# MoE 2's first block of weights converted beside the last six attention chunks and kept in DRAM; first tokens transposed beside MoE 1's last steps

## The chip, the cores and the metric

One core of one Trainium2 chip runs the program. The metric is the device time of one execution in microseconds. The kernel uses TensorE (PE, with weight loads shown as PEld), VectorE (DVE), ScalarE (ACT), GpSimd (POOL) and the DMA queue that SyncE (SP) issues.

## The reference, cut to what matters

A linear-attention recurrence over 768 tokens for 4 batches of 8 heads of width 40, and then two feed-forward stages (called MoE 1 and MoE 2) over the 3072 resulting tokens of width 320. The weights `w_in`, `w_a`, `w_b` and `w_out` arrive as 64-bit floats, the rest as 32-bit.

```python
for t in range(S):
    y[:, :, t] = np.einsum('bhd,bhde->bhe', rt, state)
    Sa = np.einsum('bhde,bhe->bhd', state, at)
    state = state * wt - np.einsum('bhd,bhe->bhde', Sa, bt) + np.einsum('bhd,bhe->bhde', vt, kt)
...
h = x @ w_in                                   # MoE 1, d_ff 2048
x = (h * np.clip(h + 3.0, 0.0, 6.0) / 6.0) @ w_out
...
a = x @ w_a                                    # MoE 2, d_ff 1536
b = x @ w_b
out = a * b @ w_out
```

## The kernel before, in words

**Chunks.** The recurrence is done in 12 chunks of 64 steps, all 32 heads at once. `window(j)` (L697) lists the steps of chunk j by hand: small matmuls for chunk j, preparation for chunks j + 1 and j + 2, and between them two kinds of fillers, `MOE_STEP` and `WEIGHT`. The table `MOE` (L30 on) says before which steps of each window the MoE 1 steps stand. Each window from chunk 2 on has seven `WEIGHT` slots: after `merge_y`, after `op_d`, two around `st_copy`, after the first `op_f`, after the second `op_e`, and after `xt_move`. They call `conv1.go()` while MoE 1's own weights are being converted. That ends in chunk 1, so from chunk 2 on the slots do nothing.

Inside a chunk POOL inverts a triangular system with 62 instructions (`t_solve`, L507), started by `t_start(j + 1)` in window j. Its input comes from `op_a` (L472) on PE by way of two copies on ACT and two DRAM scratch transfers (`t_load`, L496). Behind the solve POOL multiplies the next chunk's `LB` (`prep_a`, L451), which the next window's `op_a` reads. `t_store` (L524) writes the solution to DRAM and reads it back, and `merge_y`, `merge_z`, `op_b` to `op_g` use it. `prep_w` (L444) and `prep_kb` (L461) run on DVE.

**MoE 1** works on 256 tokens per chunk (`moe1_stream`, L292): eight up steps and eight down steps per chunk, a down step one place behind its up step. An up step is 16 matmuls; ACT then makes the gate `g`, DVE multiplies, and `split` (L129) makes a rounded high part on ACT (`gh`) and the remainder on DVE (`gl`). A down step is 12 matmuls that read them. Of 192 steps 171 stand in the windows and 21 remain after the last chunk.

**64-bit weights** are turned into 32-bit by `to_f32` (L89): one activation on ACT, then five operations on DVE, and `split` adds a cast on ACT and a subtract on DVE. ACT and DVE each take their work in program order.

**After the last window** (L986 on) the attention's SBUF is given up, and MoE 2's pools open in it. A piece of MoE 2's weights is 256 columns (128 x 256 values, three per 128 rows of `d_ff`) or 160 columns (two per 128 rows); `Weights2` (L746) loads two pieces ahead (`ahead`) and converts one per `go`. `BLOCK` is 3, so the first block is 15 pieces. While the remaining MoE 1 steps run, each of them from the third on is followed by `w2.go(BLOCK - 1)`, so the first block is converted there. After the seventh step `decide` and the first load of MoE 2's tokens (`load_x(0)`) are issued. After the nineteenth come `trans(0)` (six PE transposes, with ACT and DVE making high and low parts), `load_x(1)`, the next-to-last step, `trans(1)`, and the last step. `load_x(0)` and `load_x(1)` use the same buffer. Then `rest()` (L890) runs MoE 2: four blocks of three rows of `d_ff`, six groups of 512 tokens each; it converts the next block's weights one piece per step.

SP issues all DMAs in program order, so a DMA that waits holds those behind it.

Of the kernel before, what the change touches and what calls it, by code (L numbers as in the profile page):

```python
# [8 lines left out]
F32 = mybir.dt.float32  # L9
F32R = mybir.dt.float32r  # L10
I32 = mybir.dt.int32
# [10 lines left out]
NCH = S // C  # L22
NP = 16
NT = B * S
DM = H * D
# [11 lines left out]
WEIGHTS = {  # L37
    0: (0, 3, 6, 8, 10, 17, 18, 21, 22, 22, 26, 27),
    1: (1, 2, 4, 5, 10, 13, 16, 16, 33, 36)}
STORE_1 = 25  # L40
WEIGHTS_2, RANGE = 2, 7
INV_SCALE = 1.0e9

HALVES = ((0, 0), (1, 64))
# [44 lines left out]
def to_f32(nc, st, c, h, p):  # L89
    for step in f32_steps(nc, st, c, h, p):  # L90
        step()
    return h.bitcast(F32)


def attention_and_moe(ctx, tc, t, flag):
    nc = tc.nc
    pe, ve, ac, gp, sp = nc.tensor, nc.vector, nc.scalar, nc.gpsimd, nc.sync
# [5 lines left out]
    dram = ctx.enter_context(tc.tile_pool(name="dram", bufs=1, space=DRAM))  # L103
# [13 lines left out]
    wk1 = m1.enter_context(tc.tile_pool(name="wk1", bufs=2))  # L117
# [11 lines left out]
    def split(hi, lo, src, eng=nc.vector):  # L129
        ac.copy(out=hi, in_=src)  # L130
        eng.tensor_tensor(out=lo, in0=src, in1=hi.bitcast(F32), op=ALU.subtract)  # L131

    def split_tail(dst, src, eng=nc.vector):
        ac.copy(out=dst, in_=src)
        eng.tensor_tensor(out=dst[64:128], in0=src[64:128], in1=dst[64:128].bitcast(F32), op=ALU.subtract)

    wide = t["w1i"].dtype != F32
    room = {"wide": True, "free": ["xt", "xh", "xl"], "live": set(), "lent": True, "n": 0}

    def words(src, dma):  # L140
        st = wk1.tile([128, 192, 2], I32, tag="ws", name="ws", bufs=3)[:, 0:src.shape[1]]
        dma.dma_start(out=st.rearrange("q c w -> q (c w)"), in_=src.bitcast(I32))
        return st

    def from_words(st):
        cv = wk1.tile([128, 2, 192], I32, tag="cv", name="cv2", bufs=2)[:, :, 0:st.shape[1]]
        return to_f32(nc, st, cv[:, 0], cv[:, 1], st[:, :, 1])

    class Converter:

# [24 lines left out]
    class Interleaved(Converter):  # L175


        x = y = z = None
# [41 lines left out]
    def load1(src, n, sink, c0):  # L220

        slot = None
        if room["wide"]:
            slot = room["free"].pop(0)
            room["live"].add(slot)
            if slot == "GH":
                st = GH.rearrange("q a p c -> q (a p c)")[:, 0:2 * n]
                sp.dma_start(out=st if not wide else st.bitcast(I32), in_=src.bitcast(I32) if wide else src)
                st = st.bitcast(I32).rearrange("q (c w) -> q c w", w=2) if wide else st
            else:  # L230
                st = stage_load(wk1, (slot, 0, 0, 0, 0, 1), src, n, sp)
        else:
            n = min(n, 192)
            st = words(src[:, 0:n], sp) if wide else stage_load(wk1, ("ws", 0, 0, 0, 0, 3), src[:, 0:n], n, sp)

        def steps():
            if not wide:
                yield from range(6)
                w = st
            elif slot:  # L240
                room["n"] += 1
                h = wk1.tile([128, n], I32, tag=("cv", "gh")[room["n"] % 2], name="cv_h", bufs=2)
                f32_steps(nc, st, h, h, h)[0]()
                yield
                p = wk1.tile([128, n], I32, tag="gl", name="cv_p")
                for step in f32_steps(nc, st, h, h, p)[1:]:
# [448 lines left out]
    WEIGHT, MOE_STEP = "weight", "moe"  # L695

    def window(j):  # L697
# [45 lines left out]
    NM = FF2 // 128  # L743
    BLOCK = 3

    class Weights2:  # L746


        def __init__(self, pool, stpool):
            self.pool, self.stpool, self.up, self.dn = pool, stpool, {}, {}  # L750
            self.todo = [(m, i) for m in range(NM) for i in range(5)]
            self.loaded = []

        def source(self, m, i):
            cols = slice(128 * m, 128 * m + 128)
            if i < 2:
                return [t[("w2a", "w2b")[i]][:, 0:2, cols]]
            if i == 2:
                return [t["w2a"][:, 2:3, cols], t["w2b"][:, 2:3, cols]]
            return [t["w2o"][:, m:m + 1, 160 * (i - 3):160 * (i - 2)]]  # L760

        def ahead(self):
            while self.todo and len(self.loaded) < 2:
                m, i = self.todo.pop(0)
                srcs = self.source(m, i)
                n = sum(x.shape[1] * x.shape[2] for x in srcs)
                k = 2 if wide else 1
                st = self.stpool.tile([128, 512], I32, tag="ws2", name="ws2", bufs=2)[:, 0:k * n]
                o = 0
                for x in srcs:  # L770
                    w = k * x.shape[1] * x.shape[2]
                    sp.dma_start(out=st[:, o:o + w].rearrange("q (k c) -> q k c", k=x.shape[1]), in_=x.bitcast(I32))
                    o += w
                self.loaded.append((m, i, st))

        def go(self, last):

            self.ahead()
            if not self.loaded or self.loaded[0][0] > last:
                return  # L780
            m, i, st = self.loaded.pop(0)
            if wide:
                st = st.rearrange("q (c w) -> q c w", w=2)
                cv = wk1.tile([128, 2, 256], I32, tag="cv", name="cv2", bufs=2)[:, :, 0:st.shape[1]]
                w = to_f32(nc, st, cv[:, 0], cv[:, 1], st[:, :, 1])
            else:
                w = st.bitcast(F32)
            if i == 0:
                self.up[m] = self.pool.tile([128, 10, 128], F32R, tag="up2", name="up2", bufs=2 * BLOCK)
            if i == 3:  # L790
                self.dn[m] = self.pool.tile([128, 2, DM], F32R, tag="dn2", name="dn2", bufs=2 * BLOCK)
            if i < 2:
                split(self.up[m][:, 4 * i:4 * i + 2], self.up[m][:, 4 * i + 2:4 * i + 4],
                      w.rearrange("q (k c) -> q k c", k=2))
            elif i == 2:
                split_tail(self.up[m][:, 8:10], w.rearrange("q (k c) -> q k c", k=2))
            else:
                cols = slice(160 * (i - 3), 160 * (i - 2))
                split(self.dn[m][:, 0, cols], self.dn[m][:, 1, cols], w)
            self.ahead()  # L800
# [114 lines left out]
    with tc.manual_schedule():  # L915
# [52 lines left out]
        def moe_step():  # L968
            mq.pop(0)()
            while mq and mq[0] in preps:  # L970
                mq.pop(0)()

        for j in range(NCH):
            for f in window(j):
                if f == MOE_STEP:
                    if j == 1 and mq[0] in preps:
                        mq.pop(0)()
                    else:
                        moe_step()
                elif f == WEIGHT:  # L980
                    if conv1.todo or conv1.loaded or room["wide"]:
                        conv1.go()
                else:
                    f[0](*f[1:])
        at.close()
        c2 = ctx.enter_context(ExitStack())  # L986
        w2p = c2.enter_context(tc.tile_pool(name="w2", bufs=1, side="right", reuse_waits="tile"))
# [2 lines left out]
        w2 = Weights2(w2p, xr)  # L990
        load_x, trans, rest = moe2(w2, xr, lambda: left[0])
        decide = in_range()
        w2.ahead()
        n = 0
        while len(mq) > 2:
            moe_step()
            n += 1
            if n > WEIGHTS_2:
                w2.go(BLOCK - 1)
            if n == RANGE:  # L1000
                decide()
                load_x(0)
        trans(0)
        load_x(1)
        m1i.close()
        mq.pop(0)()
        trans(1)
# [221 lines left out]
```

## Time and profile before

| | us |
|---|---|
| three runs | 1315.85, 1321.88, 1313.23; median 1315.85 |
| the profiled execution | 1317.48 |
| its span, first to last instruction | 1315.7 |
| its mean granted PE clock | 0.941 of full speed |

The span is what the trace's positions count in; the profiled execution's time is 1.8 us longer than its span. Busy shares of the span: PE 84%, DVE 60%, ACT 39%, POOL 38%. PEclk is the clock that TensorE was granted as a share of its full 2.4 GHz; 0.5 is the lower level.

### The profile page before, as it was taken

The page shows a single profiled execution, that of the slowest core. Times are in us where ns is not written, and L with a number is a line of the kernel's source. Part 1 is how long each engine was busy: PE and PEld are TensorE (multiplying, and loading weights), DVE is VectorE, ACT ScalarE, POOL GpSimd, SP SyncE. Part 2 cuts the span into 40 slices and gives each one's busy share as a digit, 9 for nine tenths or more (in the row PEclk, how much of TensorE's full clock was granted, in tenths as well). Part 3 has the DMA queues.
Part 4 walks back from the last instruction along what each step waited for, and adds up shares of the span by engine and source line. Part 5 has one row for each costly group of instructions (what it writes and reads, how often), then busy time and mean ns, then how long its engine had stood idle before and what let it go on. Part 6 is the DMA issues. An engine that isn't in the chain of part 4 may idle for free.

```text
span 1315.7 us, 34806 instructions
## 1 busy us (share of the span) xinstructions
PE 1106.6 (84%) x14826; PEld 1010.3 (77%) x14826; DVE 793.0 (60%) x1371; ACT 516.7 (39%) x1087; POOL 502.1 (38%) x817
## 2 busy tenths in 40 slices
PE   1213347998999899898989999778999999999997
PEld 1213336898989889898989899777888888888886
DVE  7899867473746557373746334575765675675333
ACT  1242344454554545354544644333343232232221
POOL 4789205665858484756748570000000000000000
PEclk9999657898999899999989999988999999999999
DMA  6253251324151423323141321222220110110111
GB/s 176 49 143 99 67 161 42 98 63 100 56 133 37 114 69 92 91 61 100 56 120 36 89 59 41 64 74 88 82 74 24 35 43 26 35 43 11 40 40 44
DMA packets 128770, 94.43 MB, mean 72 GB/s; under 512 B 87040, under 2 KB 117888, under 8 KB 126592
## 3 DMA queue, kind: packets, MB, share of 16 engines
q1 hardware_dynamic: 128608, 92.14, 26.1%
q8 instruction: 118, 1.93, 0.6%
q14 instruction: 44, 0.36, 0.1%
HBM read 72.18 MB, written 19.92 MB: 70 GB/s over the span
## 4 chain that ended last, share of the span: by engine, by line
PE 45%; POOL 24%; DVE 12%; DMA 7%; issue 6%; ACT 4%; SPq 1%; POOLq 0%; DVEq 0%; ACTq 0%
PE att L847 20%; POOL TN L519 11%; POOL TT L516 10%; PE up L309 6%; PE ac L871 3%; PE ac L870 3%; PE ac L869 3%; POOL LB L454 3%; DMA TA<-scr 2%; PE att L482 1%; PE dn L329 1%; DMA scr<-AB 1%; PE dn L331 1%; PE dn L330 1%; DVE cv_p L78 1%
## 5 line engine op out<-in xcount | busy, mean ns | idle before, releaser
L516 POOL TENSOR_TENSOR TT<-TA,TN 64x31 f32<-64x31 f32 (+15 forms) x372 | 207.9, 559 | 228.5 <-DMA TA<-scr 200.1
L847 PE MATMUL att<-x2h,up 128*128 128x512 f32 x720 | 237.4, 394 | 0.0
L519 POOL TENSOR_TENSOR TN<-TN,TT 64x31 f32<-64x31 f32 (+15 forms) x372 | 218.2, 586 | 29.2
L847 PE MATMUL att<-x2l,up 128*128 128x512 f32 x432 | 170.7, 395 | 2.0 <-DVE x2l L832 2.0
L847 PEld LDWEIGHTS att<-x2h,up 128*128 128x128 f32 x720 | 135.4, 188 | 29.0
L329 PE MATMUL dn<-wo_h,gh 128*128 128x320 f32 x384 | 129.4, 337 | 17.4 <-ACT gh L130 17.4
L315 DVE SCALAR_TENSOR_TENSOR up<-g,up 128x512 f32<-128x512 f32 x96 | 66.5, 693 | 117.6 <-ACT g L314 117.6
L314 ACT ACTIVATE g<-up,bias 128x512 f32<-128x512 f32 x96 | 66.0, 687 | 167.1 <-PE up L309 164.0
L331 PE MATMUL dn<-wo_h,gl 128*128 128x320 f32 x384 | 122.7, 320 | 1.1 <-DVE gl L131 1.0
L330 PE MATMUL dn<-wo_l,gh 128*128 128x320 f32 x384 | 121.3, 316 | 0.0
L309 PE MATMUL up<-xh,wi_h 128*128 128x256 f32 x384 | 113.0, 314 | 3.1 <-ACT xh L288 3.1
L852 DVE TENSOR_TENSOR att<-att,asb 128x512 f32<-128x512 f32 x72 | 50.4, 700 | 98.0 <-PE att L847 80.8
L309 PE MATMUL up<-xh,wi_l 128*128 128x256 f32 x384 | 107.0, 298 | 0.0
L131 DVE TENSOR_TENSOR gl<-up,gh 128x512 fp32r<-128x512 f32 x96 | 66.4, 691 | 62.5 <-ACT gh L130 62.5
L130 ACT CAST gh<-up 128x512 fp32r<-128x512 f32 x96 | 56.2, 586 | 102.7 <-DVE up L315 102.7
L847 PEld LDWEIGHTS att<-x2l,up 128*128 128x128 f32 x432 | 81.2, 188 | 19.4 <-DVE x2l L832 3.5
L482 PE MATMUL att<-LB,KB 40*64 40x64 f32 x1408 | 40.8, 275 | 63.9 <-POOL LB L454 30.9
L329 PEld LDWEIGHTS dn<-wo_h,gh 128*128 128x128 f32 x384 | 74.4, 194 | 22.4 <-ACT gh L130 18.9
L869 PE MATMUL ac<-dn,g2h 128*128 128x320 f32 x288 | 89.5, 311 | 0.0
L482 PEld LDWEIGHTS att<-LB,KB 40*64 40x64 f32 x1408 | 35.4, 185 | 70.4 <-POOL LB L454 34.4
L871 PE MATMUL ac<-dn,g2l 128*128 128x320 f32 x288 | 88.6, 308 | 0.1
L870 PE MATMUL ac<-dn,g2h 128*128 128x320 f32 x288 | 88.7, 308 | 0.0
(146 smaller groups left out, 2549.4 us busy)
## 6 DMA issues: line engine op xcount, KB each, us to landing
RV<-in_rve_dram SPq DMA_DIRECT2D x24, 320.0 KB
KB<-in_kbe_dram SPq DMA_DIRECT2D x22, 320.0 KB
st<-in_w1i_dram SPq DMA_DIRECT2D x13, 384.0 KB
raw<-in_we_dram SPq DMA_DIRECT2D x24, 162.5 KB
LB<-in_ae_dram SPq DMA_DIRECT2D x24, 160.0 KB
VX<-in_vte_dram SPq DMA_DIRECT2D x24, 160.0 KB
yt<-Y SPq DMA_DIRECT2D x48, 80.0 KB
x2d<-x SPq DMA_DIRECT2D x24, 160.0 KB
```

What stands on the lines that cost most here:

```text
L309: mm(u[:, e], a_, b_, start=(n == 0), stop=(n == len(seq) - 1))
L315: ve.scalar_tensor_tensor(out=uf, in0=g, scalar=6.0, in1=uf, op0=ALU.min, op1=ALU.mult)
L329: mm(acc, gh[:, e, c0:c0 + 128], wo_h[:, m], start=(m == 0), stop=False)
L330: mm(acc, gh[:, e, c0:c0 + 128], wo_l[:, m], start=False, stop=False)
L331: mm(acc, gl[:, e, c0:c0 + 128], wo_h[:, m], start=False, stop=(m == 15))
L482: mm(pss[ab][half(c), i], KB[rows(ab), p, 64 * c:64 * c + 64], lb[rows(ab), ab, p], start=True, stop=True)
L516: eng.tensor_tensor(out=tv, in0=TA[:, 0:u, u:u + 1].to_broadcast([nr, u, n]), in1=TN[:, u:u + 1, u:32].to_broadcast([nr, u, n]), op=ALU.mult)
L519: eng.tensor_tensor(out=TN[:, 0:u, u:32], in0=TN[:, 0:u, u:32], in1=tv, op=ALU.subtract)
L847: mm(u, a_, b_, start=(n == 0), stop=(n == len(seq) - 1))
L869: mm(acc, gh[:, sl], w[:, 0], start=(i == 0), stop=False)
L870: mm(acc, gh[:, sl], w[:, 1], start=False, stop=False)
L871: mm(acc, gl[:, sl], w[:, 0], start=False, stop=(i == BLOCK - 1))
```

## The change

`WEIGHT` slots of windows 6 to 11 (`EARLY = NCH - 6`) no longer call `conv1.go()`. Of the seven slots of each of these windows the first, fourth and seventh advance a generator, `early2()`. Its first call loads piece 0; each later call converts the loaded piece, splits it into high and low parts that overwrite the loaded words, stores them to a DRAM tensor `made2`, and loads the next piece. After the windows `Weights2` reads all 15 pieces of the first block from `made2` straight into their places. The conversion loop beside MoE 1's last steps is gone, and `trans(0)` and `load_x(1)` are issued after the twelfth of these steps, not after the nineteenth. The staging tile `ws` gets 256 columns and two buffers in place of 192 columns and three, and the work tile `cv` one part in place of two.

```diff
+EARLY = NCH - 6
+WCOLS = 256
-WEIGHTS_2, RANGE = 2, 7
+RANGE = 7
...
-        st = wk1.tile([128, 192, 2], I32, tag="ws", name="ws", bufs=3)[:, 0:src.shape[1]]
+        st = wk1.tile([128, WCOLS, 2], I32, tag="ws", name="ws", bufs=2)[:, 0:src.shape[1]]
...
-        cv = wk1.tile([128, 2, 192], I32, tag="cv", name="cv2", bufs=2)[:, :, 0:st.shape[1]]
-        return to_f32(nc, st, cv[:, 0], cv[:, 1], st[:, :, 1])
+        h = wk1.tile([128, WCOLS], I32, tag="cv", name="cv2", bufs=2)[:, 0:st.shape[1]]
+        return to_f32(nc, st, h, h, st[:, :, 1])
...
+    made2 = dram.tile([BLOCK * PIECES, 128, 512], F32, name="made2")
...
+    def early2():
+
+        todo = [(m, i) for m in range(BLOCK) for i in range(PIECES)] if wide else []
+        st = load2(wk1, "ws", 2 * WCOLS, *todo[0]) if wide else None
+        yield
+        for n, (m, i) in enumerate(todo):
+            w = f32_2(st)
+            c = w.shape[1]
+            hi, lo = st[:, 0:c].bitcast(F32R), st[:, c:2 * c].bitcast(F32R)
+            if i == 2:
+                split_tail(hi, w)
+                sp.dma_start(out=made2[n, :, 0:c].bitcast(I32), in_=st[:, 0:c])
+            else:
+                split(hi, lo, w)
+                sp.dma_start(out=made2[n, :, 0:2 * c].bitcast(I32), in_=st)
+            if n + 1 < len(todo):
+                st = load2(wk1, "ws", 2 * WCOLS, *todo[n + 1])
+            yield
...
+            while wide and self.todo[0][0] < BLOCK:
+                m, i = self.todo.pop(0)
+                self.room(m, i)
+                src = made2[PIECES * m + i]
...
+                sp.dma_start(out=dst.bitcast(F32), in_=src)
...
+        first2, early = early2(), [0] * NCH
...
+                elif f == WEIGHT and j >= EARLY:
+                    early[j] += 1
+                    if early[j] in (1, 4, 7):
+                        next(first2, None)
...
+        for _ in first2:
+            pass
         at.close()
...
-        w2.ahead()
         n = 0
         while len(mq) > 2:
             moe_step()
             n += 1
-            if n > WEIGHTS_2:
-                w2.go(BLOCK - 1)
             if n == RANGE:
                 decide()
                 load_x(0)
-        trans(0)
-        load_x(1)
+            if n == RANGE + 5:
+                trans(0)
+                load_x(1)
```

## Rows read from the trace of the kernel before

**Rows 1.** The page, part 2: PE's busy tenths in 40 slices.
```profile
PE   1213347998999899898989999778999999999997
```
**Rows 2.** Windows view: stretch, PE, PEld, DVE, ACT, POOL busy (instructions), PEclk, DMA share, GB/s.
```profile
742.00:827.00 85.00, 85.00 (x1609) 81.17 (x1608) 32.96 (x50) 38.13 (x67) 32.73 (x62) 1.00 0.19 48
...
831.00:904.00 73.00, 53.05 (x307) 49.31 (x307) 49.36 (x122) 25.11 (x56) 0.00 (x0) 0.82 0.24 72
...
682.00:742.00 60.00, 56.78 (x1085) 53.77 (x1085) 34.63 (x47) 30.08 (x64) 40.03 (x66) 0.97 0.31 74
...
830.00:835.00 5.00, 5.00 (x39) 5.00 (x39) 2.24 (x4) 1.84 (x4) 0.00 (x0) 1.00 0.63 184
```
**Rows 3.** Waits from 831 to 904 us: total us, times, longest.
```profile
PE dn L329 <- ACT gh L130: 16.5, 7, 6.3
```
**Rows 4.** Timeline of PE: start, length, instruction, [idle before and releaser].
```profile
827.30 0.28 PE L309 MATMUL up<-xh,wi_h 128*128 128x256 f32 x1
...
829.22 0.31 PE L329 MATMUL dn<-wo_h,gh 128*128 128x320 f32 x1
...
830.98 0.28 PE L309 MATMUL up<-xh,wi_h 128*128 128x256 f32 x1
...
838.93 0.42 PE L329 MATMUL dn<-wo_h,gh 128*128 128x320 f32 x1 [0.43 <-ACT gh L130]
...
843.14 0.28 PE L309 MATMUL up<-xh,wi_h 128*128 128x256 f32 x1
...
851.61 0.64 PE L329 MATMUL dn<-wo_h,gh 128*128 128x320 f32 x1 [6.27 <-ACT gh L130]
...
890.34 0.82 PE L828 MATMUL att<-ident,xin 128*128 128x128 f32 x6
...
904.17 0.63 PE L847 MATMUL att<-x2h,up 128*128 128x512 f32 x1
```
**Rows 5.** Timeline of ACT: the cast that ends a weight piece.
```profile
845.37 0.40 ACT L130 CAST up<-cv 128x256 fp32r<-128x256 f32 x1 [2.07 <-DVE cv L86]
```
**Rows 6.** The chain that ended last, in order of time: start, length, what.
```profile
668.48 2.16 POOL LB L454
...
728.43 2.15 POOL LB L454
```
**Rows 7.** PE's waits from 682 to 742 us, the only row.
```profile
PE att L482 <- POOL LB L454: 3.2, 2, 1.9
```
**Rows 8.** Timeline of ACT, chunk 9: the evictions of `merge_z`.
```profile
691.54 1.20 ACT L562 ACTIVATE AB<-att 32x512 f32<-32x512 f32 x2 [1.90 <-PE att L559]
```
**Rows 9.** Timeline of POOL: first and last instructions of solves.
```profile
91.32 0.34 POOL L516 TENSOR_TENSOR TT<-TA,TN 64x31 f32<-64x31 f32 x1
...
134.61 0.25 POOL L519 TENSOR_TENSOR TN<-TN,TT 64x31 f32<-64x31 f32 x1
...
688.97 0.34 POOL L516 TENSOR_TENSOR TT<-TA,TN 64x31 f32<-64x31 f32 x1 [14.89 <-DMA TA<-scr]
...
747.39 0.26 POOL L516 TENSOR_TENSOR TT<-TA,TN 64x31 f32<-64x31 f32 x1 [13.47 <-DMA TA<-scr]
...
784.64 0.25 POOL L519 TENSOR_TENSOR TN<-TN,TT 64x31 f32<-64x31 f32 x1
```
**Rows 10.** DVE groups by form, 91.3 to 134.9 us: busy us, mean ns, idle before.
```profile
L447 DVE TENSOR_TENSOR_SCAN W<-raw,seg 128x260 f32<-128x260 f32 x4 | 3.7, 926 | 0.0
...
L263 DVE TENSOR_TENSOR wi_t<-cv_h,wi_t 64x384 fp32r<-64x384 f32 x1 | 0.9, 854 | 0.0
```
**Rows 11.** DVE groups by form, 689 to 728.5 us.
```profile
L465 DVE TENSOR_TENSOR KB<-KB,rw 128x512 f32<-128x512 f32 x4 | 3.4, 860 | 1.0 <-DMA KB<-in_kbe_dram 1.0
...
L447 DVE TENSOR_TENSOR_SCAN W<-raw,seg 128x260 f32<-128x260 f32 x3 | 2.4, 785 | 0.0
```
**Rows 12.** Tile `ws`, 831 to 904 us: ns min/median/max, first and last start.
```profile
L80 DVE SCALAR_TENSOR_TENSOR cv<-cv,ws x15: 324/425/428, 840.8 to 894.4; 128x256 int32<-128x256 int32 x9, 128x160 int32<-128x160 int32 x6
...
L772 SPq DMA_DIRECT2D ws<-in_w2a_dram x7: 341/378/527, 830.7 to 891.3; - x7
```

More of the change, by code (lines that the diff above doesn't have):

```diff
@@ L233, in load1 @@
             n = min(n, 192)
-            st = words(src[:, 0:n], sp) if wide else stage_load(wk1, ("ws", 0, 0, 0, 0, 3), src[:, 0:n], n, sp)
+            st = words(src[:, 0:n], sp) if wide else stage_load(wk1, ("ws", 0, 0, 0, 0, 2), src[:, 0:n], n, sp)
         def steps():
@@ L744, in attention_and_moe, with source2, load2, f32_2 @@
     BLOCK = 3
+    PIECES = 5
+    made2 = dram.tile([BLOCK * PIECES, 128, 512], F32, name="made2")
+    def source2(m, i):
+        cols = slice(128 * m, 128 * m + 128)
+        if i < 2:
+            return [t[("w2a", "w2b")[i]][:, 0:2, cols]]
+        if i == 2:
+            return [t["w2a"][:, 2:3, cols], t["w2b"][:, 2:3, cols]]
+        return [t["w2o"][:, m:m + 1, 160 * (i - 3):160 * (i - 2)]]
+    def load2(pool, tag, room_, m, i):
+        srcs = source2(m, i)
+        k = 2 if wide else 1
+        st = pool.tile([128, room_], I32, tag=tag, name=tag, bufs=2)[:, 0:k * sum(x.shape[1] * x.shape[2] for x in srcs)]
+        o = 0
+        for x in srcs:
+            w = k * x.shape[1] * x.shape[2]
+            sp.dma_start(out=st[:, o:o + w].rearrange("q (k c) -> q k c", k=x.shape[1]), in_=x.bitcast(I32))
+            o += w
+        return st
+    def f32_2(st):
+        if not wide:
+            return st.bitcast(F32)
+        st = st.rearrange("q (c w) -> q c w", w=2)
+        h = wk1.tile([128, WCOLS], I32, tag="cv", name="cv2", bufs=2)[:, 0:st.shape[1]]
+        return to_f32(nc, st, h, h, st[:, :, 1])
+    def early2():
[6 more added lines that the diff above has]
+            hi, lo = st[:, 0:c].bitcast(F32R), st[:, c:2 * c].bitcast(F32R)
+            if i == 2:
+                split_tail(hi, w)
[6 more added lines that the diff above has]
+            yield
     class Weights2:
@@ L750, in __init__, with room @@
             self.pool, self.stpool, self.up, self.dn = pool, stpool, {}, {}
-            self.todo = [(m, i) for m in range(NM) for i in range(5)]
+            self.todo = [(m, i) for m in range(NM) for i in range(PIECES)]
             self.loaded = []
[L754 to L760, printed above, removed]
+            while wide and self.todo[0][0] < BLOCK:
+                m, i = self.todo.pop(0)
+                self.room(m, i)
+                src = made2[PIECES * m + i]
+                if i < 2:
+                    dst, src = self.up[m][:, 4 * i:4 * i + 4], src.rearrange("q (k c) -> q k c", c=128)
+                elif i == 2:
+                    dst, src = self.up[m][:, 8:10], src[:, 0:256].rearrange("q (k c) -> q k c", c=128)
+                else:
+                    dst = self.dn[m][:, :, 160 * (i - 3):160 * (i - 2)]
+                    src = src[:, 0:320].rearrange("q (k c) -> q k c", k=2)
+                sp.dma_start(out=dst.bitcast(F32), in_=src)
+        def room(self, m, i):
+            if i == 0:
+                self.up[m] = self.pool.tile([128, 10, 128], F32R, tag="up2", name="up2", bufs=2 * BLOCK)
+            if i == 3:
+                self.dn[m] = self.pool.tile([128, 2, DM], F32R, tag="dn2", name="dn2", bufs=2 * BLOCK)
         def ahead(self):
@@ L764, in ahead @@
                 m, i = self.todo.pop(0)
[L765 to L774, printed above, removed]
+                self.loaded.append((m, i, load2(self.stpool, "ws2", 512, m, i)))
         def go(self, last):
@@ L781, in go @@
             m, i, st = self.loaded.pop(0)
[L782 to L791, printed above, removed]
+            w = f32_2(st)
+            self.room(m, i)
             if i < 2:
```

## The prediction

> **What bounds the kernel now.** I read the page's forty slices first. TensorE is near full from slice 8 on, except for a dip at slices 26 to 28 (busy tenths 7, 7, 8; each slice is 32.9 us) [rows 1]. The windows view puts numbers on the two stretches around it: from 742 to 827 us, the last two chunks, PE is busy all 85 us, but from 831 to 904 us, the last 21 steps of MoE 1, it is busy 53.05 of 73 us and its granted clock averages 0.82 [rows 2]. The waits of that stretch have one owner: the down steps waited 16.5 us for the cast `gh` [rows 3]. PE's timeline shows the pattern. Undisturbed, a down step takes 829.22 to 830.98, that is 1.76 us, and an up step 827.30 to 829.22, 1.92 us. With weight pieces between a gate's cast and its input, the first down step of the last chunk comes 6.27 us late, and its matmuls then take 0.64 us, not 0.31: the lower of the clock's two levels [rows 4]. On ACT a piece holds the in-order queue: after its first activation (as long as its cast, 0.40 us) ACT stands 2.07 us until DVE's fifth operation is done and then casts for 0.40 us, 2.9 us in all [rows 5].
>
> In the chunks before, something else ends last. The chain of waits runs through a ring: POOL's `LB` product, `op_a` on PE, an up step, the scratch DMAs into `TA`, then POOL's solve until the next `LB` product. One turn is 668.48 to 728.43, 59.95 us [rows 6]. PE is 95% busy there (56.78 of 60 us [rows 2]) but waits 3.2 us a chunk, only for `LB` [rows 7]. So in chunks 6 to 9 PE has 3.2 us to give away, and POOL and the ring have nothing.
>
> **The change, part by part.**
>
> *1. Fifteen pieces leave the tail.* I rebuild PE's order without them. Up to 843.14 + 1.92 = 845.06 nothing changes. Then follow down 0 (1.76 us, plus 0.9 us because only one up step stands between its input and itself; the same kind of spot costs 0.43 us at 838.93 [rows 4]), so 847.7; six up steps (11.5 us); seven down steps (12.3 us); and the transposes of the first two token blocks, twice 0.82 us [rows 4]. Sum: 873.1. MoE 2's first matmul stood at 904.17 [rows 4], so it comes 31.0 us earlier. That matmul and the next few ran at the lower clock (0.63 us for one); without an idle stretch ahead I count another 0.7 us. Together 31.7 us.
> What hides the rest of this stretch: ACT and DVE keep only the gates; their chain from an up step's end to `gl` fits in the 3.68 us of the next pair, as it does without a wait at 829 us. If that cover failed, a pair would cost some 0.4 us more, 3 us in all.
>
> *2. Fifteen reloads.* They are issued on SP right behind the last tokens' own load: 15 x 0.38 us [rows 12] = 5.7 us of SP, 2.95 MB. The tokens stand ahead of them, the store of MoE 1's chunk 10 and the first load of `x2d` behind. At the 184 GB/s that the queue reached at 830 to 835 us [rows 2] they need 16 us and are in by 847; the first transposes come at about 855, MoE 2 at 873. Cost 0. If they only went at the stretch's mean of 72 GB/s [rows 2] they would take 41 us, and the first transposes would be 17 us late. I take the peak row, because it was measured for the same kind of load back to back, and the mean only shows what was asked for.
>
> *3. The first transposes in the loop.* The six matmuls are counted above. `load_x(1)` shares their buffer and can start at about 856; `trans(1)` stands at about 870, so there are 14 us for one load. Cost 0; before, it cost an idle stretch. The first pieces of the second block are no longer loaded ahead, but only in MoE 2's second step; their conversion stands behind that step's evictions and the next tokens' casts on ACT, and what it makes is needed five groups later: cost 0, at most one wait for a load, on ACT alone.
>
> *4. The pieces in the chunks: PE.* Per chunk three slots are used, after `merge_y`, ahead of `op_f` and behind `xt_move`; the first `next` only loads, so chunk 6 gets two pieces, chunks 7 to 10 three, chunk 11 one. Behind `merge_y` ACT's next work is the evictions of `merge_z`, which started after 1.90 us of idle [rows 8]; a stay of 2.9 us makes them 1.0 us late, and `op_c` with them. At the other two slots ACT and DVE have idle time of that size and PE other work. So PE arrives about 1 to 1.5 us later at `op_a`, where it waits 3.2 us anyway: cost 0 in chunks 6 to 9. In chunks 10 and 11 no wait is left [rows 2]: two first slots, at most 2 x 1.0 us; I take 0.5. If all fifteen stays landed on the chain it would be 15 x 2.9 = 43 us.
>
> *5. The pieces in the chunks: POOL.* This is the term that decides. Every piece puts four DVE operations with two inputs in SBUF (`L80`, `L84`, `L86` and the split's subtract; 0.425 us each at 256 columns [rows 12]) beside POOL's solve, and POOL is in the ring. The trace shows three solves of the same 62 instructions. With next to no such operations it takes 747.39 to 784.64 + 0.25, 37.50 us. With seven more of them (four `L465`, three `L447`, 5.8 us [rows 11]) it runs from 688.97 [rows 9] to the `LB` product at 728.43 [rows 6], 39.46 us: 2.0 us more, 0.28 us per operation. Beside MoE 1's conversion, with 35 of them in 30.1 us (thirteen groups, the first and the last of them in [rows 10]), it takes 91.32 to 134.86, 43.54 us: 6.0 us more, 0.17 us per operation [rows 9]. So a piece costs POOL 4 x 0.17 = 0.7 to 4 x 0.28 = 1.1 us; by busy time (6.0 / 30.1 = 0.20 and 2.0 / 5.8 = 0.34, times 1.7 us) it is 0.34 to 0.58 us. I take 0.7, the middle. Eleven pieces stand beside a solve that the ring waits for (two in chunk 6, three each in 7, 8, 9): 7.7 us, bounds 3.7 and 12.3. The solve of chunk 10 is the last, and its end is followed by steps that wait for ACT: 0.
> The Trainium skill (SBUF — State Buffer, "Who interferes with whom") says that a VectorE instruction with two SBUF inputs and a GpSimd one that reads SBUF exclude each other, and that the loser blocks for the whole instruction. The rows agree that there is a price, but 0.17 to 0.28 us is a fraction of those operations' lengths (about 0.85 us). By the rule at its fullest the term would be 18.7 us in place of 7.7.
>
> *6. The pieces in the chunks: SP.* Each slot's store waits for the split, with the next load behind it. At the third slot `load_rv`, the next chunk's loads and `t_store` are queued behind; 2 x 0.38 us a chunk over four chunks is 3.2 us at most. PE waits for none of what these bring [rows 7], so I take 0.
>
> *7. Two `ws` buffers in place of three, one `cv` half in place of two.* Only seven pieces of MoE 1 use them before; a load there may wait for one conversion. Between 0 and 0.6 us; I take 0.
>
> Sum: -31.7 + 7.7 + 0.5 = -23.5 us. The profiled execution took 1317.48 us, so 1294.0 on its own scale; the median of the three runs, 1315.85, is 1.6 us lower, and so is the forecast: **1292.4 us**.
>
> **The rivals.**
> - *The chunks hide everything* (POOL's loss stays near 0, or PE's later arrival at `op_a` saves what POOL loses, since the up step there runs at the lower clock after the wait): 1292.4 - 7.7 = 1284.7. For it: DVE is only 58% busy in a chunk (34.63 of 60 us [rows 2]). Against: the three solves.
> - *POOL loses the whole length of each such operation*: 4 x 0.425 = 1.7 us a piece, 11 x 1.7 = 18.7, so 1303.4. For it: the gap between 37.50 and 39.46 exists at all. Against: 35 operations of 0.86 us cost 6.0 us, not 30.
> - *The reloads are slow* and the first transposes wait: +17, so 1309. Against: 184 GB/s in the row.
> - *Slower: ACT's stay lands on the ring or on PE each time.* Place: ACT's queue at the three slots. Price: 2.9 us x 15 = 43 us against 31.7, so 1315.85 + 11.8 = 1328. It decides from 31.7 / 15 = 2.1 us a piece. For it: a stay of 2.9 us in an in-order queue, which did cost the tail 6.27 us once; Against: in the tail several pieces stood together, here one stands alone among steps that leave 3.2 us a chunk.
> - *It doesn't do what it says*: 18 slots for 16 calls leave no remainder for after the chunks, so only if the tail were bound by something else: 1315.
>
> **How the numbers follow.** A measurement of this kernel can tell about 1%, 13.2 us, from no change. Chances: forecast 0.57, all hidden 0.21, full lock 0.11, slow reloads 0.04, slower 0.05, nothing 0.02. Faster by over 1% means below 1302.7: the forecast, all hidden, and half of the full lock, 0.57 + 0.21 + 0.06 = 0.84. Within 1%: the other half, slow reloads, nothing, 0.11. Slower 0.05. The range reaches from just under the hidden case, 1283, to the full lock, 1304; its ends also cover part 5's bounds (1288 to 1297) with parts 4, 6 and 7 at their dearest.
>
> **What would show it.** In the changed profile: no wait on `gh` over 1 us between the last chunk and MoE 2, that stretch some 42 us long, at full clock; solves of chunks 7 to 9 about 2 us longer than 39.5 and a ring of about 62 us; PE still waiting for `LB` only. Wrong would be: solves as before (then 1285), new waits on `AB` or `VX` in chunks 10 and 11, or on `xin` or the reloaded weights ahead of MoE 2.

## The result, and the profile after

The kernel after takes 1301.39 us (median of 8 runs, 1299.54 to 1306.14), the kernel before 1315.06 us (8 runs): 0.9896 of it, 95% interval 0.9873 to 0.9918. That is 13.7 us faster; the forecast had 23.5. The change's profiled execution took 1300.71 us, its span is 1298.9 us. The page's slices of PE (the kernel after):

```profile
PE   1213347998999898989899999999999999999997
```

The dip of [rows 1] at slices 26 to 28 is gone. The windows view of the kernel after, with columns as in [rows 2] (one turn of the ring, the last two chunks, and MoE 1's last steps):

```profile
690.00:752.00 62.00, 57.59 (x1094) 53.81 (x1094) 43.81 (x65) 32.16 (x70) 40.10 (x66) 1.00 0.38 94
...
754.00:839.00 85.00, 81.66 (x1486) 77.36 (x1486) 40.47 (x71) 39.27 (x73) 34.53 (x62) 0.98 0.23 62
...
845.00:888.00 43.00, 41.91 (x312) 40.61 (x311) 19.30 (x33) 15.71 (x26) 0.00 (x0) 1.00 0.34 104
```

PE's waits of the last of these stretches, which answer to [rows 3]:

```profile
PE dn L331 <- ACT gh L132: 0.6, 2, 0.4
...
```

PE's timeline there, the first tokens' transposes and MoE 2's first matmul, which answer to the last two of [rows 4]:

```profile
869.76 0.82 PE L872 MATMUL att<-ident,xin 128*128 128x128 f32 x6
...
888.04 0.39 PE L891 MATMUL att<-x2h,up 128*128 128x512 f32 x1
```

The tail did what was forecast: 16.5 us of waiting for `gh` became 0.6, PE is busy 41.91 of 43 us at full clock, and MoE 2's first matmul takes 0.39 us in place of 0.63. In the chunks DVE has 9 us more to do in a turn (43.81 against 34.63), and PE, which waited for nothing but `LB` there [rows 7], now waits for other engines too. Its waits from 690 to 752 us, the turn that answers to that of [rows 7]:

```profile
PE att L484 <- POOL LB L456: 2.5, 2, 1.9
PE att L639 <- DVE GH L618: 0.5, 2, 0.3
PE att L655 <- ACT VX L592: 0.5, 1, 0.5
...
```

**Where the time went.** I cut the ring into two parts by POOL's timeline: a *solve*, from the first to the last of its 62 instructions, and the *leg* from its end to the next solve's start (`LB` product, `op_a`, `t_store`, `t_load`). The pieces stand beside the five solves of chunks 6 to 10 and in the legs between them; the table adds up these five solves and the five legs that lead into them. The two rows in which one such solve begins and ends in the kernel after (chunk 8) show how each is read; the bracket says what POOL waited for:

```profile
636.32 0.25 POOL L518 TENSOR_TENSOR TT<-TA,TN 64x31 f32<-64x31 f32 x1 [18.53 <-DMA TA<-scr]
...
676.20 0.25 POOL L521 TENSOR_TENSOR TN<-TN,TT 64x31 f32<-64x31 f32 x1
```

So this solve took 40.13 us, and the leg before it ran from 612.3, the end of the solve before, to 636.32, 24.0 us. Read so in every profile (us; MoE 2's start by the chain that ended last; the times are medians, the ratios to the kernel before on the same chip):

| kernel | five solves, chunks 6 to 10 | legs into them | last solve to MoE 2 | MoE 2 starts | time | ratio |
|---|---|---|---|---|---|---|
| before | 195.2 | 100.5 | 119.5 | 904.4 | 1315.06 | 1 |
| after | 200.1 | 107.0 | 90.6 | 888.2 | 1301.39 | 0.9896 |
| *first chip* | | | | | | |
| e1, no pieces | 195.7 | 98.5 | 88.2 | 871.3 | 1285.19 | 0.9771 |
| e2, transfers alone | 195.5 | 101.0 | 91.1 | 876.8 | 1291.77 | 0.9824 |
| e3, no stores | 201.2 | 100.8 | 90.3 | 877.3 | 1295.05 | 0.9849 |
| e4, third slot earlier | 197.8 | 129.4 | 94.4 | 909.6 | 1321.18 | 1.0041 |
| *second chip* | | | | | | |
| f1, store kept back | 198.6 | 114.9 | 93.9 | 895.8 | 1307.26 | 0.9924 |
| f2, two slots, 8 chunks | 197.5 | 107.6 | 90.9 | 887.1 | 1298.00 | 0.9850 |
| f3, transposes late | 199.9 | 104.3 | 92.6 | 886.6 | 1301.52 | 0.9882 |
| f4, DVE additions alone | 204.8 | 103.0 | 86.0 | 882.3 | 1298.11 | 0.9852 |
| *third chip* | | | | | | |
| g1, `xt` loads later | 199.6 | 105.1 | 90.0 | 885.6 | 1293.94 | 0.9834 |
| g2, g1 and f2 | 198.1 | 98.0 | 89.4 | 879.1 | 1287.07 | 0.9771 |
| g3, after once more | 200.0 | 105.4 | 95.0 | 888.1 | 1296.91 | 0.9847 |
| g4, f2 once more | 198.1 | 101.7 | 90.3 | 881.6 | 1296.40 | 0.9850 |

The kernel after gains 28.9 us behind the last solve (119.5 to 90.6) and 0.6 in MoE 2, and gives back 4.9 in the solves, 6.5 in the legs and 1.3 ahead of the first of these legs: 16.8 us, the difference of the spans.

One plain limit of this table: the same kernel's ratio was 0.9896 (0.9873 to 0.9918) at first and 0.9847 (0.9824 to 0.9869) on the third chip, the legs of one kernel differ by up to 6 us between two profiles (f2 and g4), and its last stretch by 4.4 (after and g3). So times are compared within one chip's group, and a leg counts where the queue's rows say why it is long.

### The profile page after: what moved, and what is told of

It is laid out like the page before. It is cut to its first block, busy times and chain, and to the rows that moved or that the text cites. A ratio compares the mean times of both kernels' runs of the same rounds, so it can differ in the third digit from the quotient of the medians.

```text
span 1298.9 us, 34813 instructions
## 1 busy us (share of the span) xinstructions
PE 1103.0 (85%) x14826; PEld 1006.5 (77%) x14826; DVE 807.8 (62%) x1371; ACT 518.0 (40%) x1087; POOL 507.6 (39%) x817
## 4 chain that ended last, share of the span: by engine, by line
PE 43%; POOL 19%; DVE 13%; DMA 11%; ACT 6%; issue 5%; SPq 2%; POOLq 0%; DVEq 0%; ACTq 0%
PE att L891 21%; POOL TN L521 8%; POOL TT L518 8%; PE up L311 6%; PE ac L915 3%; PE ac L914 3%; PE ac L913 3%; POOL LB L456 2%; DMA scr<-AB 2%; DMA TA<-scr 2%; DMA KB<-in_kbe_dram 2%; PE att L484 2%; DVE rw L451 1%; DMA st<-in_w1o_dram 1%; PE dn L333 1%
## 5 line engine op out<-in xcount | busy, mean ns | idle before, releaser
L521 POOL TENSOR_TENSOR TN<-TN,TT 64x31 f32<-64x31 f32 (+15 forms) x372 | 222.4, 598 | 29.2
L484 PE MATMUL att<-LB,KB 40*64 40x64 f32 x1408 | 38.1, 261 | 59.5 <-POOL LB L456 26.2
L451 DVE RECIPROCAL rw<-W 128x256 f32<-128x256 f32 x48 | 84.2, 1753 | 3.2 <-ACT sq L461 0.2
L484 PEld LDWEIGHTS att<-LB,KB 40*64 40x64 f32 x1408 | 32.8, 172 | 65.9 <-POOL LB L456 29.5
```

The costliest lines, as they stand in the source:

```text
L451: ve.reciprocal(out=rw, in_=w[:, :, 1:65])
L484: mm(pss[ab][half(c), i], KB[rows(ab), p, 64 * c:64 * c + 64], lb[rows(ab), ab, p], start=True, stop=True)
L521: eng.tensor_tensor(out=TN[:, 0:u, u:32], in0=TN[:, 0:u, u:32], in1=tv, op=ALU.subtract)
```

## What lengthens a leg

SP's queue at the chunk's end, in the timeline of the kernel before (start, length, line, transfer; the solve ends at 609.7):

```profile
606.21 0.83 SPq L435 DMA_DIRECT2D RV<-in_rve_dram  x2
...
608.23 0.67 SPq L427 DMA_DIRECT2D LB<-in_ae_dram  x2
609.70 0.31 SPq L532 DMA_DIRECT2D n<-TN  x1
...
612.38 0.32 SPq L534 DMA_DIRECT2D n<-TA  x1
616.09 0.32 SPq L538 DMA_DIRECT2D NY<-n  x1
...
618.57 0.49 SPq L540 DMA_DIRECT2D AB<-n  x1
621.47 1.98 SPq L502 DMA_DIRECT2D scr<-AB  x4
625.27 0.47 SPq L505 DMA_DIRECT2D TA<-scr  x1
```

SP is through with the loads 0.8 us before the solve ends, so `t_store`'s first store goes out 0.03 us behind it. Its last reload is out at 619.06; `t_load`'s `scr` store starts at 621.47, 2.4 us later, because it waits for `AB` from ACT. These two gaps, 0.8 and 2.4 us, are all the slack that SP has. The same queue in the kernel after, one chunk further on (the solve ends at 676.45):

```profile
673.36 0.39 SPq L680 DMA_DIRECT2D xt<-yt  x1
673.79 1.12 SPq L682 DMA_DIRECT2D xt<-yt  x2
675.00 0.54 SPq L789 DMA_DIRECT2D made<-ws  x1
675.58 1.42 SPq L767 DMA_DIRECT2D ws<-in_w2o_dram  x1
677.05 0.74 SPq L437 DMA_DIRECT2D RV<-in_rve_dram  x2
...
679.41 0.31 SPq L534 DMA_DIRECT2D n<-TN  x1
...
681.83 1.13 SPq L536 DMA_DIRECT2D n<-TA  x1
687.35 0.32 SPq L540 DMA_DIRECT2D NY<-n  x1
...
689.85 0.48 SPq L542 DMA_DIRECT2D AB<-n  x1
690.38 2.15 SPq L504 DMA_DIRECT2D scr<-AB  x4
695.36 0.46 SPq L507 DMA_DIRECT2D TA<-scr  x1
```

The piece's store and the next load stand between `xt_move` and the loads. The store doesn't wait (it goes out 0.1 us behind `xt_move`), but `RV` now follows `xt_move` by 2.1 us in place of 0.1. And `xt_move` itself is later against the solve's end (3.1 us ahead of it, before 5.1). The first store now goes out 2.96 us behind the solve's end, and `scr` right behind the last reload (689.85 + 0.48), with nothing left to wait for. The stores also land later: from the last store's issue to the first reload SP stands 4.4 us (682.96 to 687.35), against 3.4. The leg is 22.8 us, 3.5 more than the one shown from the kernel before: 2.1 by the later `scr`, 1.2 because `scr` then takes 5.0 us to the load of `TA` in place of 3.8, 0.2 by the rest.

Why `xt_move` is late is read in the chain of waits that leads to it (start, length, what; the kernel after):

```profile
661.49 0.45 DVE ws L80
...
665.55 0.43 DVE ws L133
...
666.01 0.33 SPq L792
...
667.75 1.91 DMA yt<-Y
669.66 0.67 DVE Y L640
...
670.67 2.67 DMA yt<-Y
...
673.36 0.39 SPq L680
```

The piece of the *fourth* slot holds DVE from 661.49 to 665.98, and the first half of `Y` stands behind it. Its store to `yt` stands on SP behind the piece's store and loads, the second half of `Y` waits for that store, and `xt_move` for the second half's. In the kernel before, the two halves of `Y` in the same chunk (the solve ends at 668.41) lay 7.2 us apart, with nothing of a piece ahead of them:

```profile
653.25 0.68 DVE L638 TENSOR_TENSOR Y<-att,W 104x512 f32<-104x512 f32 x1
...
660.47 0.68 DVE L638 TENSOR_TENSOR Y<-att,W 104x512 f32<-104x512 f32 x1
```

So two of the three pieces lengthen this leg: the fourth slot's by way of `Y`, the seventh's by its place on SP.

## The experiments

Theory Q: what SP's queue and the transfers do lengthens the chunks. Theory P: the conversion's work on ACT and DVE does, beside POOL and PE.

**e1, e2, e3: the halves of a piece alone.**

In e1 no piece is made, and the fifteen reloads read one filled piece:

```diff
-        for n, (m, i) in enumerate(todo):
...
+        fill()
         yield
...
-                src = made2[PIECES * m + i]
+                src = made2[0]
```

In e2 the same slots load and store filler, and nothing is converted:

```diff
-            w = f32_2(st)
-            c = w.shape[1]
+            c = st.shape[1] // 2
...
-                split_tail(hi, w)
...
-                split(hi, lo, w)
```

In e3 each piece is loaded and converted, and not stored; the reloads are as in e1:

```diff
-                sp.dma_start(out=made2[n, :, 0:c].bitcast(I32), in_=st[:, 0:c])
...
-                sp.dma_start(out=made2[n, :, 0:2 * c].bitcast(I32), in_=st)
```

> Leaves out the conversion of the first block altogether: the chunks hold no piece, and the fifteen reloads read one filler block of the same size, so the output is not the reference's. It shows the tail's gain alone. Both theories: the tail gives the 31 us of the rebuilt order, so about 1284 us, the solves of chunks 6 to 9 back at 39.4 us and the time from a solve's end to the next solve's start back at 19 to 21.5 us. If it comes out near 1295, the tail itself gave less than was worked out.

> Leaves out the conversion in the chunks but keeps each slot's store and load, with filler data of the same size (output not the reference's). Theory Q (SP's queue and the transfers at the chunk's end hold back the scratch transfers of the ring): about 1284 + 6 = 1290 us, with the legs from solve to solve stretched as in the changed kernel (24.0 and 22.8 us at chunks 8 and 9). Theory P (DVE's and ACT's work beside POOL and PE is what costs): 1284 us, legs as before.

> Keeps each slot's load and conversion but leaves out the stores; the reloads read one filler block (output not the reference's). Theory Q: the solves keep their 1 to 1.5 us each, the legs shrink since SP no longer waits for the split behind which the next chunk's loads stand: about 1289 us. Theory P: nearly all of the loss stays, 1299 to 1301 us.

Measured: 1285.19 us (ratio 0.9771, 0.973 to 0.9812), 1291.77 (0.9824, 0.9782 to 0.9867) and 1295.05 (0.9849, 0.9807 to 0.9891). Without pieces the stretch behind the last solve is 88.2 us against 119.5, 31.3 less, and solves and legs are as before: the tail's term is right, and all that is missing is lost in the chunks. Both halves cost, 6.6 and 9.9 us by the medians (3.9 and 4.6 by the profiled executions, so the sizes are loose); every run of either is slower than every run of e1. The solves separate them: with transfers alone 195.5 us, the same as without pieces; with the conversion 201.2. So POOL pays for the conversion and for nothing else, and neither Q nor P alone holds. The legs grow by 2.5 and 2.3 us in the halves, which is no more than two profiles differ, but by 8.5 in the whole. SP's queue says why: in the four legs behind the first, `t_store`'s first store goes out 1.9, 0.6, 0.3 and 0.03 us behind the solve's end in e2, 0.4, 0.5, 0.03 and 0.02 in e3, and 1.8, 1.8, 3.0 and 0.4 in the kernel after.

**e4: the third slot earlier**, so that no store stands at the chunk's end.

```diff
-                    if early[j] in (1, 4, 7):
+                    if early[j] in (1, 4, 5):
```

> The third piece of each chunk is moved from the slot behind the last step's token load to the fifth slot, behind the first op_f; nothing is left out. Theory Q: its store and load no longer stand ahead of the next chunk's loads and of t_store, so the legs go back to about 20 us: 1296 us. Theory P: the same work beside the same solve, 1301 us.

Measured: 1321.18 us (ratio 1.0041, 1.0025 to 1.0058), a miss for both theories. The waits from 650 to 720 us:

```profile
PE att L639 <- DVE GH L618: 8.9, 1, 8.9
...
ACT cv L79 <- DMA ws<-in_w2b_dram: 4.8, 1, 4.8
```

Slot 5's load is issued only when slot 4's piece is done. ACT stands 4.8 us for it, the piece's DVE operations stand behind ACT, the mask `GH` behind them, and PE waits 8.9 us for `GH`. The legs are 27 us. It tells nothing of Q or P; it shows what a piece costs once its load doesn't have a slot's distance.

**f1: store and next load kept back** until the next chunk's `t_start` has been issued.

```diff
+            if n % 3 == 1:
+                yield
+            k = c if i == 2 else 2 * c
+            sp.dma_start(out=made2[n, :, 0:k].bitcast(I32), in_=st[:, 0:k])
...
+                if j > EARLY and f[0] is (op_kbt if j + 1 < NCH else op_b) and f[-1] == (0 if j + 1 < NCH else 1):
+                    next(first2, None)
```

> The changed kernel, but the piece converted behind xt_move keeps its store, and the load of the next piece, back until the next chunk's t_load and t_start have been issued. Nothing is left out. Theory Q (what SP holds behind that store makes the legs between solves longer): the legs of chunks 7 to 10 fall from 21.1, 24.0, 22.8, 19.5 us to about 20 each, solves stay at 39.5 to 40.9, and the time is 1301.4 - 6.5 = 1295. Theory P (the conversion's work on ACT and DVE makes them longer, wherever the store stands): legs and time as in the changed kernel, 1301. A miss for both: slower than 1303, the later load then holds ACT at the next chunk's first slot.

Measured: 1307.26 us (0.9924, 0.9902 to 0.9946), the case named as a miss for both. A wait of ACT from 608 to 674 us:

```profile
ACT cv L79 <- DMA ws<-in_w2a_dram: 7.3, 1, 7.3
```

The load moved with the store arrives 7.3 us late for the next chunk's first slot; `merge_z`'s eviction stands behind it on ACT, and PE waits 5.9 us for that. `RV` follows `xt` by 1.65 us again, as before, but in the two longest legs, 25.5 and 27.2 us, `xt` itself is now issued 0.1 and 1.1 us behind the solve's end, because all that comes before it is late.

**f2: two slots in eight chunks.**

```diff
-EARLY = NCH - 6
+EARLY = NCH - 8
-                    if early[j] in (1, 4, 7):
+                    if early[j] in (1, 4):
```

> The changed kernel, but with two pieces a chunk over eight chunks (slots 1 and 4 of chunks 4 to 11), none behind xt_move. Nothing is left out. Theory Q: without that slot no store stands ahead of the chunk's end on SP, legs near 20 us, time 1301.4 - 6.5 = 1295, or up to 1 lower because two pieces a chunk fit better into PE's wait for LB. Theory P (a price by the piece, about 1 us): thirteen pieces stand ahead of the last solve in place of eleven that count in the ring, 1302 to 1303.

Measured: 1298.0 us (0.985, 0.983 to 0.9871), by the ratio Q's number. But the legs of 23.5, 22.9 and 22.2 us spoke against Q's reason: with no store at the chunk's end, `t_store` was still 2.9 us late in the first two of them, because `xt` was issued only 1.4 and 1.6 us ahead of the solve's end in place of 5 (in the third, `scr` took 5.3 us to land in place of 3.8). And on the third chip (g4) the same kernel's median is only 0.5 us below that of the kernel after.

**f3: the first transposes at their old place.**

```diff
-            if n == RANGE + 5:
-                trans(0)
-                load_x(1)
+        trans(0)
+        load_x(1)
```

> The changed kernel, but the first tokens are turned, and the second load of tokens issued, behind the loop over MoE 1's steps, where the kernel before had them. Nothing is left out. If part 3 is worth what the rebuilt PE order gives (an idle stretch before the transposes at most, the six steps that stand between them hide the rest): 1301.4 + 0.5 to 2.5, so 1302 to 1304. Rival: the move carries a good part of the tail's gain, because MoE 2's start then waits for the evictions and casts of both token blocks: 1306 or more.

Measured: 1301.52 us (0.9882, 0.9863 to 0.99), between the two results of the kernel after. The kernel after didn't run on this chip, so the times tell neither 1 us nor the rival's 4.6. PE's waits from 843 to 887 us do:

```profile
PE att L872 <- DMA xin<-x2d: 1.3, 1, 1.3
```

The kernel after doesn't have this wait, and the others of this stretch are no longer than there. So the move is worth 1.3 us, within the forecast of 0.5 to 2.5; the rival, that it carries a good part of the tail's gain, falls.

**f4: four DVE additions a piece, and nothing else** (on top of e1).

```diff
+            for _ in range(4):
...
+                ve.tensor_tensor(out=h.bitcast(F32), in0=st[:, 0:c].bitcast(F32), in1=st[:, c:2 * c].bitcast(F32), op=ALU.add)
```

> The kernel without any pieces in the chunks (1285.2 measured), plus, at the same slots and in the same widths, four DVE additions a piece with both inputs in SBUF; no ACT work, no loads, no stores; the weights of MoE 2's first block are one filler piece, so the output is not the reference's. Port theory (these operations, and not ACT's stay or the transfers, lengthen POOL's solves): solves of chunks 7 to 9 at 40.7 to 41.0 us as in the kernel that converts without storing, against 39.5 without pieces, and the time 1285.2 + 11 x 0.45 = 1290. Rival (the price of a conversion is ACT's stay and the DVE queue): solves at 39.5 and 1285 to 1286. At a full lock, 1.5 us a piece: 1300 or more.

Measured: 1298.11 us (0.9852, 0.9829 to 0.9875): more than the port theory asked, less than a full lock (12.9 us above e1 by the medians; e1 ran on another chip, and by the ratios it is 10.7). The solve beside chunk 8, and DVE's additions beside it (group by form: busy us, mean ns, idle before):

```profile
631.62 0.55 POOL L518 TENSOR_TENSOR TT<-TA,TN 64x31 f32<-64x31 f32 x1 [14.70 <-DMA TA<-scr]
...
673.61 0.25 POOL L521 TENSOR_TENSOR TN<-TN,TT 64x31 f32<-64x31 f32 x1
```

```profile
L793 DVE TENSOR_TENSOR cv<-ws 128x256 f32<-128x256 f32 x12 | 6.4, 595 | 0.0
```

42.24 us with twelve additions, against 39.5 in the four solves of the same profile that have none (39.53, 39.69, 39.61, 39.24): 2.7 us, 0.23 each. Over the five solves it is 9.1 us more than in e1 for 14 x 4 additions, 0.16 each, just under the prediction's 0.17 to 0.28. No ACT work, load or store is in it: DVE's operations alone lengthen POOL's solves. MoE 2 starts 11.0 us later than in e1: 9.1 by the solves, 4.5 by the legs, and 2.6 less elsewhere. So SP's queue isn't all that lengthens a leg: in these legs `t_store`'s first store is never more than 0.03 us late. Ahead of `scr` SP waits there for `AB` (545 to 760 us):

```profile
SPq L504 <- ACT AB L487: 20.1, 7, 5.8
```

`scr` goes out 12.8, 12.8, 12.8 and 12.3 us behind the solve's end in the four legs behind the first, against 11.9, 11.9, 12.9 and 11.7 in e1. Why `AB` comes later is open.

**g1 to g4: the loads of `xt_move`, with and without the third slot, on one chip.** In g1 and g2 the three loads are issued inside the next chunk's `t_store`, between its stores and its reloads.

```diff
-            ... + on(j > 1, (t_store, j))
+            ... + on(j > 1, (t_store, j) + ((lambda: xt_move(j - 1),) if j > EARLY else ()))
-            + on(j, (xt_move, j)) + [WEIGHT]
+            + on(j, (xt_move, j) if j < EARLY or j == NCH - 1 else (idle,)) + [WEIGHT]
```

> The changed kernel, but from the seventh chunk on the three loads of xt_move are issued in the next chunk, inside t_store, between its three stores and the loads that wait for these to land; only the last chunk's stay. Nothing is left out. Theory Q (on SP, loads that wait for the late Y stand ahead of t_store, whose stores then start 1.8 to 3.0 us after the solve's end in place of 0.03): the first of t_store's stores comes back to within 0.5 us of the solve's end, the legs of 21.1, 24.0 and 22.8 us become 20 to 21, and the ratio to the kernel before falls by some 6 us, from 0.9896 to 0.985. Theory P (PE, ACT and DVE set the legs): legs and ratio as in the changed kernel. In between: the piece behind the old place still holds SP by its store, then only about half of the 6 us come back.

> Two pieces a chunk over eight chunks, and the loads of xt_move inside the next chunk's t_store from the fifth chunk on. Nothing is left out. Theory Q: here nothing of a piece stands ahead of t_store and nothing that waits for Y does, so its first store stands within 0.1 us of the solve's end in every chunk, the legs of 23.5, 22.9 and 22.2 us become about 20.5, and the time is 5 to 7 us under the kernel with two slots alone, 0.980 of the kernel before. Theory P: as with two slots alone, 0.985.

> The changed kernel itself, for a comparison with the other three on one chip: both theories 0.9896 of the kernel before, with the interval 0.9873 to 0.9918.

> The kernel with two slots over eight chunks once more, on the same chip as the changed kernel: 0.985 of the kernel before and about 6 us under the changed kernel if the first comparison, made on another chip, holds; equal to it if that was the chip.

Measured, in this order: 1293.94 us (0.9834, 0.9812 to 0.9855), 1287.07 (0.9771, 0.9749 to 0.9792), 1296.91 (0.9847, 0.9824 to 0.9869) and 1296.40 (0.985, 0.9827 to 0.9873). Against g3, neither edit alone makes a difference that the intervals can tell (3.0 and 0.5 us less by the medians), and both together take 9.8 us. The legs point the same way, less sharply: 105.4 us in g3, 105.1 in g1, 101.7 in g4 (107.6 in f2, the same kernel), 98.0 in g2, which is that of the kernel without pieces (98.5). The profiled executions divide it otherwise: g4's is 6.7 us below g3's, g2's only 2.7 below g4's. So the 9.8 us of both together are clear, and how they divide between the two edits isn't. In g1 the third slot's store still stands ahead of the loads, and the first store of `t_store` is 1.8 us late in two chunks; in g4, where `xt` still waits for `yt` ahead of the loads, it is 3.0 us late in the leg into chunk 6's solve and 0.8 to 0.9 in two others. SP's queue in g2 (the solve ends at 672.75):

```profile
667.70 0.69 SPq L437 DMA_DIRECT2D RV<-in_rve_dram  x2
...
672.76 0.67 SPq L429 DMA_DIRECT2D LB<-in_ae_dram  x2
673.53 0.31 SPq L534 DMA_DIRECT2D n<-TN  x1
...
677.06 0.31 SPq L536 DMA_DIRECT2D n<-TA  x1
677.43 0.41 SPq L680 DMA_DIRECT2D xt<-yt  x1
...
679.15 0.53 SPq L540 DMA_DIRECT2D NY<-n  x1
...
684.10 1.99 SPq L504 DMA_DIRECT2D scr<-AB  x4
```

`RV` is out 4.4 us before the solve ends, the `xt` loads lie in the time in which SP waited for `t_store`'s landing (from 545 to 760 us 11.9 us before, 17.4 after, 13.5 in g4; none in g2, where the first reload follows the last store by 1.8 us), and `scr` goes out at 11.35 us behind the solve's end, where it stood at 11.8 before and at 13.9 in the kernel after. The first store is still 0.8 us late: the `LB` load ahead of it now waits for the matmuls that free its buffer. Q's number for g2 (0.980) was too small a gain, its number for g1 (0.985) was met only because the kernel after stands at 0.9847 on this chip; its reason for g1 was wrong, since the store that stays holds the queue without `xt`. Whether the moved `xt` loads would shorten the legs of a kernel without pieces too wasn't tried. g2 is the fastest of the kernels that leave nothing out: 29.0 us under the kernel before on its chip, and 9.8 under the change.

## Why the prediction was right or wrong

The time, 1301.39 against 1292.4, lies inside the range, near its slow end; the sign and the largest term were right. That it lies inside is in part luck: the range reaches that far for the full lock, which the runs refute, and for parts 4 to 7 all at their dearest; and part 5 was 2.8 us too dear, which hid as much of part 6's 6.5. On the profiled executions' scale the sum missed by 6.7 us (1300.71 against 1294.0): 2.1 in the tail, 6.5 in the legs, 1.3 ahead of them and 0.1 in MoE 2, less 2.8 in the solves and the 0.5 of part 4. Of the signs that it named, those of the tail came true; the solves of chunks 7 to 9 grew by 1.6, 0.7 and 0.05 us where 2 was said, and PE didn't wait for `LB` only. Term by term:

- *Part 1, the tail, -31.0 and -0.7: right.* 31.3 without pieces (e1); 28.9 in the kernel after, where PE also waits 2.7 us for `NY` in chunk 11, behind a solve that ended late. MoE 2 itself gained 0.6 against 0.7.
- *Part 2, the reloads, 0: nothing against it.* PE waits for no reload ahead of MoE 2; the rival that made them slow would show there.
- *Part 3, the transposes, 0: right.* No wait for `xin` is left; at the old place it is 1.3 us (f3).
- *Part 4, PE in the chunks, +0.5: the cover held on PE, not for `Y`.* PE's wait for `LB` in four successive turns fell from 4.6, 3.7, 3.6 and 3.2 us to 4.0, 2.3, 2.6 and 2.5, so PE came 0.6 to 1.4 us later, where 1 to 1.5 was said, and had time left. New waits of 1.5 to 2.7 us a turn came on PE beside it. What the part left out is `Y`: it said that at the second and third place ACT and DVE have idle time for a piece, but at the fourth slot the first half of `Y` stands right behind the piece on DVE (the piece's last operation starts at 665.55, `Y` at 665.90).
- *Part 5, POOL, +7.7: right in kind, too dear per piece and wrong on one solve.* The five solves grew by 4.9 us for fourteen pieces, 0.35 a piece (0.39 in e3, 0.65 in f4, where the four operations stand back to back), where 0.7 was taken. And the solve beside chunk 10, counted as 0, grew by 1.8 us and ended that much later: it counted like the others, since the chain that ended last runs from its last instruction through `t_store` and `NY` to the steps of chunk 11. The price by busy time, 0.34 to 0.58 a piece, which the prediction worked out and set aside, held for the pieces of the change.
- *Part 6, SP's queue, 0: the step that failed.* The prediction bounded it by the issue time, 0.76 us a chunk or 3.2 us in all, and set it to 0 because "PE waits for none of what these bring". But POOL does: `t_store` is queued behind them on SP, `t_load` behind `t_store`, and the next solve behind `t_load`. The legs grew by 6.5 us; in the leg shown the issue alone took 2.1 us. PE then waited too, in the turn of the longest leg (583 to 645 us, the kernel after):

```profile
PE att L550 <- DMA NY<-n: 1.3, 1, 1.3
```

That the third piece's store and `xt_move`'s late loads, taken out together, are worth the legs is shown by g2: the legs are back at 98.0 us and the time falls by 9.8 us. (g2 also has its pieces spread over eight chunks; its solves, 198.1 us, are no shorter than g4's.) That neither edit alone would do isn't shown: g1 and g4 differ from g3 by less than the intervals can tell. How much of `Y`'s lateness comes from ACT's part of the piece, how much from DVE's longer operations and how much from the store on SP wasn't separated.
- *Part 7, the buffers, 0:* the 1.3 us lost ahead of the first of these legs are no more than such a stretch differs between two profiles (the kernel after reached the same point at 490.5 and, once more, at 487.6 us).

Of the rivals, the full lock (1.7 us a piece) falls: the largest price measured is 0.65 a piece over five solves, 0.9 beside a single one (f4, chunk 8). The Trainium skill (SBUF — State Buffer, "SBUF: two separate sides") says that the loser blocks for the whole instruction, and that a DMA and a compute operation don't slow each other. The runs agree that a transfer takes no part (the solves of e2 take 195.5 us, those of e1 195.7). They don't show a block of POOL for a whole VectorE operation; they show that both engines pay. Beside the solve of chunk 8 the piece's DVE operations took (groups by form, the kernel after):

```profile
L82 DVE SCALAR_TENSOR_TENSOR cv<-cv,ws 128x256 int32<-128x256 int32 x2 | 1.5, 758 | 0.1
L86 DVE SCALAR_TENSOR_TENSOR ws<-ws 128x256 f32<-128x256 uint32 x2 | 1.5, 748 | 0.1
L88 DVE TENSOR_TENSOR cv<-cv,ws 128x256 f32<-128x256 f32 x2 | 1.2, 598 | 0.1
L85 DVE TENSOR_SCALAR ws<-cv 128x256 int32<-128x256 int32 x2 | 1.0, 495 | 0.1
```

against 0.425 us for the first of them in the tail [rows 12], where POOL is idle, and 0.426 for the two below it. So most of the price fell on DVE, 0.17 to 0.33 us for each of these three, and about 0.1 an operation on POOL. The fourth row has one input in SBUF, wasn't counted by the prediction, and is longer too (296 ns in the tail). The prediction priced a stay by the tail's uncontended rows: at the fourth slot of chunk 8 ACT stood 3.93 us for DVE, not 2.07 [rows 5].

"All hidden" (1284.7) is what the change would have been without any price in the chunks: e1 measured 1285.19. The slower rival, ACT's stay on the ring each time, didn't come at the change's slots; it did come in e4 and f1, where a piece's load was late, for some 19 us (e4 against the change, by the ratios 1.0041 and 0.9896).

## What to carry to other kernels

Work that is moved off a tail into a ring's slack has to be priced on every queue that it passes, and a DMA queue's slack is read like an engine's: take the time from an issue to what released it (0.8 us ahead of the first store, 2.4 ahead of `scr` here) and see whether anything that waits now stands ahead of it. "No engine waits for what these transfers bring" is not enough; ask what is queued behind them. And follow a load that waits back to what makes it late: here it was the piece of an earlier slot, on another engine. When two things hold the same queue, taking either away may show nothing that can be told: test them together.

## What was not expected of the hardware

A VectorE operation with two inputs in SBUF beside POOL's solve becomes up to 1.8 times as long (758 ns against 425), and four of them to a piece, with no other work, cost the solves 0.16 us each. And the ratio of the same two kernels differed between two comparisons by more than its intervals, 0.9896 against 0.9847, so that a difference of half a per cent is only told within one chip's group.
